# One more digit level in the expert routing, and all weight subtractions on GpSimd

## The chip, the cores and the metric

The kernel runs on one core of one Trainium2 chip. The metric is device time in microseconds from launch to end. A core has TensorE (matmuls, here PE, with PEld for its weight loads), VectorE (DVE), ScalarE (ACT), GpSimd (POOL) and SyncE (SP), which run their own queues in order and meet through semaphores; data sits in SBUF, matmuls write to PSUM, and sixteen DMA engines move data to and from HBM.

## The reference

Three stages, all in 32-bit floats. Attention over 4 batches, 8 heads, 768 positions with 64 dimensions, where a query sees the four first positions and the 128 last ones. Then a mixture of three projections, `h = max(x@w1, x@w2, x@w3)` and `h @ w_out` over 3072 tokens. Then eight experts of equal capacity, and the routing of tokens to them is what the change touches:

```python
logits = x @ w_gate                    # 3072 tokens, 8 experts
order = np.argsort(-logits.flatten())
for idx in order:                      # best bid first
    tok, e = idx // 8, idx % 8
    if assigned[tok] >= 0 or counts[e] >= cap: continue     # cap = 384
    assigned[tok] = e; counts[e] += 1
for e in range(8):
    mask = assigned == e
    out[mask] = np.maximum(x[mask] @ w1[e], 0) @ w2[e]      # 512 -> 1024 -> 512
```

## The kernel before

Matmuls run on the fp32r type, and exactness comes from splitting: each operand is a high part (a rounded copy, made by ScalarE) and a low part (source less high part), and a product is three matmuls, high by high, high by low and low by high. All high and low copies of weights are made in the kernel.

The attention and the first mixture (Attn and Moe1) fill the time to about 661 us. Then eight experts follow (Moe2). An expert works in eight slices of 128 hidden units. For each slice, `weights` (line 541) loads a quarter-megabyte slice of w1 into the staging tile sa and one of w2 into sb (two buffers each, loads issued on SyncE), ScalarE writes the high parts wah and wbh, and a subtraction on line 551 writes the low parts wal and wbl, into rings of six (`nring`). The counter `s.cv` sends the subtractions by turns to GpSimd and to VectorE: w1's (wal) always goes to GpSimd, w2's (wbl) to VectorE. Line 604 has the twelve matmuls of the first layer (into mm), lines 607 and 608 split its result into hh (ScalarE) and hl (VectorE), and line 597 has the nine matmuls of the second layer (into acc), one slice behind. After the eighth slice, three indirect DMAs on GpSimd's queue write the rows out (line 616).

The routing (Route) runs one expert at a time, in a chain. A phase finds the expert that fills up next, given what each free token bids for its best expert. It does so by a search over the 32 bits of the bid's sortable key, in digit levels, highest first: `SH` holds the shifts of the levels and `NZ` the number of values of each. In one level, VectorE compares each token's digit with all thresholds (`compare`, line 398, tile th, 24 columns of tokens by NZ thresholds), TensorE counts by expert in 24 small matmuls (`count`, line 404, weights ohr, into rc), VectorE compares the counts with the room left (met, line 448), a matmul merges the experts (line 450), VectorE adds up the digit (hit, line 451) and makes the next level's z (line 453), with w (line 444, line 445 in the last level) computed beside. Behind the levels, lines 454 to 498 settle who is taken (t1b, vt and others), and `slots` (line 505) turns the result into a list of rows idx. Then `fetch` (line 554) gathers the rows with three indirect DMAs on GpSimd's queue, and `turn` (line 565) transposes them on TensorE (pt, line 25). The first level's compare and count of a phase stand in `bids` (line 405), most of it for the first phase ahead of 661 us; seven phases run in all, six of them from 661 us on, and the eighth expert takes what is left (`last`).

What runs when is set by the framework's scheduler, which orders each engine's queue once, when the kernel is built. The routing steps are marked to go ahead of the work around them (by 300 or 400 places, `s1` and `s2`), so their instructions stand between the matmuls of the first experts. A step for expert n+2 is written ahead of expert n, and the transposes of expert n+1 ahead of slice 5 of expert n. No queue changes its order at run time.

Of the kernel before, what the change touches and what calls it, by code (L numbers as in the profile page):

```python
# [22 lines left out]
def f32(ap): return ap.bitcast(FT)  # L23
# [3 lines left out]
class Attn:  # L27
    def __init__(s, tc, q,k,v, keep, consts, pst, psp, pss, psv, work):
        s.tc=tc; s.nc=nc=tc.nc; s.q,s.k,s.v=q,k,v
        s.pst,s.psp,s.pss,s.psv,s.w=pst,psp,pss,psv,work  # L30
        jp=work.tile([128,128],I32,name="jp",tag="qs0",bufs=2)
        nc.gpsimd.iota(jp,pattern=[[1,128]],base=0,channel_multiplier=-1)
        s.ident=keep.tile([128,128],FR,name="ident")
        nc.vector.tensor_scalar(s.ident,jp,0.0,None,op0=OP.is_equal)
        s.ca=consts.tile([128,2,128],U8,name="ca")
        nc.vector.tensor_scalar(s.ca[:,0,:],jp,0.0,None,op0=OP.is_le)
        nc.vector.tensor_scalar(s.ca[:,1,:],jp,0.0,None,op0=OP.is_gt)
        s.ul=consts.tile([128,2,128],BF,name="ul")
        nc.vector.tensor_scalar(s.ul[:,0,:],jp,0.0,None,op0=OP.is_lt)
        nc.vector.tensor_scalar(s.ul[:,1,:],jp,0.0,None,op0=OP.is_ge)  # L40
        s.negs=consts.tile([128,2,4],FT,name="negs"); nc.vector.memset(s.negs,NEG)

        s.ps=consts.tile([128,160],FR,name="psn"); nc.vector.memset(f32(s.ps),0.0)
        s.vn=consts.tile([16,2,64],FT,name="vns"); nc.vector.memset(s.vn,0.0)
        s.vk=[]
        for i in range(2):
            t=consts.tile([128,2,128],FR,name=f"vk{i}"); nc.vector.memset(f32(t),0.0); s.vk.append(t)
        s.ks=consts.tile([128,2,64],FT,name="kss"); nc.vector.memset(s.ks,0.0)
        s.kf=[]; s.kz=[s.zeros([consts.tile([128,4,132],FR,name=f"kz{h}") for h in range(2)])]
        t=consts.tile([1,1],FT,name="one"); nc.vector.memset(t,0.0)  # L50
        nc.scalar.activation(t,t,AF.Exp)
        s.n=0; s.no=('kh0','kh1'); s.early=[]
        s.extra=None
        s.acc=lambda u: False
# [298 lines left out]
class Route:  # L353

    SH=(25,18,12,6,0); NZ=(128,128,64,64,64)
    M=128
    def __init__(s,tc,LG,pool,work,ps,cap=384):
        s.tc=tc; s.nc=nc=tc.nc; s.LG=LG; s.w=work; s.ps=ps; s.cap=cap  # L360
        c=pool; n=len(s.SH); V=nc.vector
        io=work.tile([128,192],FT,name="te")[:,0:128]
        nc.gpsimd.iota(io,pattern=[[1,128]],base=0,channel_multiplier=0,allow_small_or_imprecise_dtypes=True)
        s.thr=c.tile([128,128],BF,name="thr")
        V.tensor_copy(s.thr,io)
        pi=c.tile([128,1],FT,name="pcol"); s.pcol=pi
        nc.gpsimd.iota(pi,pattern=[[0,1]],base=0,channel_multiplier=1,allow_small_or_imprecise_dtypes=True)
        s.ones=c.tile([128,128],BF,name="onesb"); V.memset(s.ones,1.0)
        s.scale=c.tile([128,128],BF,name="scaleb"); V.memset(s.scale,128.0*8/s.M)
        s.tri=c.tile([128,128],BF,name="trib")  # L370
        V.tensor_scalar(s.tri,io,pi,1.0,op0=OP.is_ge,op1=OP.subtract)
        s.rank8=c.tile([128,8],FT,name="rank8")
        V.tensor_scalar(s.rank8,io[:,0:8],-1.0,8.0,op0=OP.mult,op1=OP.add)
        s.io8=c.tile([128,8],FT,name="io8"); V.tensor_copy(s.io8,io[:,0:8])
        s.io3=c.tile([128,3],FT,name="io3"); V.tensor_copy(s.io3,io[:,0:3])
        s.cp=c.tile([128,24,2],FT,name="cp")
        V.tensor_copy(s.cp[:,:,0],pi.to_broadcast([128,24]))
        V.tensor_copy(s.cp[:,:,1],io[:,0:24])

        po=c.tile([128,1],I32,name="pown"); pf=c.tile([128,1],FT,name="pownf")  # L380
        V.tensor_copy(po,pi); V.tensor_scalar(po,po,7,None,op0=OP.bitwise_and); V.tensor_copy(pf,po)
        s.own=c.tile([128,8],FT,name="own"); V.tensor_scalar(s.own,s.io8,pf,None,op0=OP.is_equal)
        s.sh=c.tile([128,n-1,24],I32,name="shifts"); s.mk=c.tile([128,n-1,24],I32,name="masks"); s.z24=c.tile([128,24],FT,name="z24"); V.memset(s.z24,0.0)
        for l in range(1,n):
            V.memset(s.sh[:,l-1,:],s.SH[l])
            V.memset(s.mk[:,l-1,:],127 if s.NZ[l]==128 else 63)
        s.R=c.tile([128,8],FT,name="room"); V.memset(s.R,float(cap))
        s.RP=c.tile([128,1],FT,name="roomp"); V.memset(s.RP,float(cap))
        s.UA=c.tile([128,24],FT,name="taken"); V.memset(s.UA,0.0)
        s.ASG=c.tile([128,24,8],BF,name="asg"); V.memset(s.ASG,0.0)  # L390
        s.ML=c.tile([128,24,8],FT,name="ml")
# [13 lines left out]
    def bids(s,r=(0,24),first=False):  # L405

        nc=s.nc; n=len(s.SH); V=nc.vector; a,b=r; m=b-a; C=slice(a,b)
        if a==0:
# [10 lines left out]
        V.tensor_tensor(key,key,bid.bitcast(I32),op=OP.bitwise_xor)  # L419
        V.tensor_scalar(s.D0[:,C],key,s.SH[0],s.NZ[0]-1,op0=OP.logical_shift_right,op1=OP.bitwise_and)  # L420
        V.tensor_copy(s.z[:,C],s.D0[:,C][:,:,None].to_broadcast([128,m,2]))
# [11 lines left out]
    def phase(s,bids=True):  # L433
        nc=s.nc; n=len(s.SH); V=nc.vector; M=s.M
        if bids: s.bids()
# [99 lines left out]
class Moe2:  # L535

    def __init__(s,tc,w1,w2,x2d,out,wpool,act,main,mm,acc,pt,ident,nring):
        s.tc=tc; s.nc=tc.nc; s.w1=w1; s.w2=w2; s.x2d=x2d; s.out=out
        s.wp=wpool; s.act=act; s.main=main; s.ng=0; s.mm=mm; s.acc=acc; s.pt=pt; s.ident=ident; s.nring=nring
        s.scat=[]; s.cv=0  # L540
    def weights(s,ev,f):
        nc=s.nc
        a=s.wp.tile([128,4,128],FT,name="sa",bufs=2); b=s.wp.tile([128,512],FT,name="sb",bufs=2)
        nc.sync.dma_start(a,s.w1[bass.ds(ev,1)].rearrange("a (k p) n -> p (a k) n",p=128)[:,:,f*128:(f+1)*128])
        nc.sync.dma_start(b,s.w2[bass.ds(ev,1)].rearrange("a f n -> (a f) n")[f*128:(f+1)*128,:])
        r=[]
        for nm,src in (("wa",a),("wb",b)):
            h=s.wp.tile(list(src.shape),FR,name=nm+"h",bufs=s.nring); l=s.wp.tile(list(src.shape),FR,name=nm+"l",bufs=s.nring)
            nc.scalar.activation(h,src,AF.Copy)  # L549
            s.cv+=1  # L550
            (nc.vector if s.cv%2==0 else nc.gpsimd).tensor_tensor(l,src,f32(h),op=OP.subtract)  # L551
            r.append((h,l))
        return r
    def fetch(s,idx,first=None):
# [191 lines left out]
```

## Time and profile before

| | us |
|---|---|
| median of 3 runs (1047.61 to 1052.12) | 1052.06 |
| the profiled execution | 1053.32 |
| its span, first to last instruction | 1051.5 |
| busy: TensorE / weight load / VectorE / ScalarE / GpSimd | 978.9 / 893.3 / 774.3 / 512.4 / 414.5 |
| mean granted TensorE clock | 0.977 of full |

Times are from the span's start. Matmuls are pipelined and the end of each is modelled, so a matmul's own duration overlaps the next one's, and what one costs is read from the distance of starts. A share of busy time is a mean over stages that have different limits, so the rows below are taken by stage. A wait is put down to the semaphore that came last.

### The profile page before, as it was taken

How to read it: one execution, taken by the hardware profiler on the slowest of the kernel's cores; microseconds unless marked ns; L12 is line 12 of the kernel's file. 1: busy time of each engine (PE TensorE's matmuls, PEld its weight loads, DVE VectorE, ACT ScalarE, POOL GpSimd, SP SyncE). 2: the span in 40 equal slices, each digit the busy share in tenths (PEclk: the TensorE clock that was granted, in tenths of full speed). 3: DMA queues.
4: the chain of work that ended last, by engine and by line, in shares of the span. 5: the costliest groups of instructions: out<-in, count | busy, mean ns of one | idle time of the engine just before them, and what ended most of it. 6: DMA issues, size and time to landing. Idle time of an engine off the chain costs nothing. (4 is left out here: it accounts for less than half of the span.)

```text
span 1051.5 us, 18670 instructions
## 1 busy us (share of the span) xinstructions
PE 978.9 (93%) x6682; PEld 893.3 (85%) x6682; DVE 774.3 (74%) x1822; ACT 512.4 (49%) x1166; POOL 414.5 (39%) x355
## 2 busy tenths in 40 slices
PE   6889999989999999999999999898978999899997
PEld 4658789989999999999999898777767778688896
DVE  6789976688888888988976526877868888763330
ACT  5775563577666666666664211423323333344441
POOL 2666635234444434444344000415334254272431
PEclk8899999999999999999999999989999999999999
DMA  5564421231121121122110000424234253364530
GB/s 136 132 169 138 141 58 49 70 100 46 42 56 47 45 71 41 39 70 46 42 41 2 1 1 31 148 83 146 91 110 153 71 160 102 120 207 119 156 100 31
DMA packets 148845, 89.61 MB, mean 85 GB/s; under 512 B 90160, under 2 KB 133680, under 8 KB 148752
## 3 DMA queue, kind: packets, MB, share of 16 engines
q1 hardware_dynamic: 144048, 74.39, 25.4%
q0 software_dynamic: 3840, 12.45, 3.6%
q10 hardware_dynamic: 864, 1.57, 0.4%
q8 instruction: 53, 0.87, 0.3%
q14 instruction: 40, 0.33, 0.1%
HBM read 74.76 MB, written 13.76 MB: 84 GB/s over the span
## 5 line engine op out<-in xcount | busy, mean ns | idle before, releaser
L551 POOL TENSOR_TENSOR wal<-sa,wah 128x512 fp32r<-128x512 f32 x64 | 89.1, 1393 | 204.1 <-ACT wah L549 198.3
L202 POOL TENSOR_TENSOR L<-A_w,H 128x768 fp32r<-128x768 f32 x46 | 87.2, 1895 | 140.2 <-ACT H L201 121.0
L317 PE MATMUL mm<-woh,hh 128*128 128x260 f32 (+1 forms) x288 | 83.3, 292 | 2.2 <-DVE LG L320 1.1
L549 ACT ACTIVATE wah<-sa 128x512 fp32r<-128x512 f32 x64 | 40.4, 631 | 91.6 <-PE mm L604 50.4
L317 PE MATMUL mm<-woh,hl 128*128 128x260 f32 (+1 forms) x288 | 82.4, 290 | 2.4 <-DVE hl L334 1.2
L317 PE MATMUL mm<-wol,hh 128*128 128x260 f32 (+1 forms) x288 | 82.3, 287 | 0.0
L298 DVE TENSOR_TENSOR hm<-mm,hm 128x384 f32<-128x384 f32 x96 | 53.1, 553 | 37.7 <-PE mm L295 36.7
L597 PE MATMUL acc<-wbl,hh 128*128 128x512 f32 x192 | 78.3, 408 | 0.0
L597 PE MATMUL acc<-wbh,hh 128*128 128x512 f32 x192 | 78.0, 406 | 0.1
L597 PE MATMUL acc<-wbh,hl 128*128 128x512 f32 x192 | 78.0, 406 | 0.0
L551 DVE TENSOR_TENSOR wbl<-sb,wbh 128x512 fp32r<-128x512 f32 x64 | 52.2, 818 | 32.8 <-ACT wbh L549 31.4
L549 ACT ACTIVATE wbh<-sb 128x512 fp32r<-128x512 f32 x64 | 40.3, 630 | 68.0 <-PE acc L597 55.7
L608 DVE SCALAR_TENSOR_TENSOR hl<-mm,hh 128x384 fp32r<-128x384 f32 x64 | 35.4, 554 | 50.9 <-ACT hh L607 47.6
L295 PE MATMUL mm<-xh,w0h 128*128 128x384 f32 x192 | 67.8, 353 | 2.3 <-DVE hm L298 1.1
L295 PE MATMUL mm<-xh,w1h 128*128 128x384 f32 x192 | 66.7, 347 | 1.7 <-DVE hm L298 0.9
L295 PE MATMUL mm<-xl,w0h 128*128 128x384 f32 x192 | 65.8, 342 | 0.8 <-DVE xl L285 0.8
L295 PE MATMUL mm<-xh,w2h 128*128 128x384 f32 x192 | 66.0, 344 | 0.3 <-ACT hm L297 0.3
L295 PE MATMUL mm<-xh,w2l 128*128 128x384 f32 x192 | 65.1, 339 | 0.0
L295 PE MATMUL mm<-xh,w1l 128*128 128x384 f32 x192 | 65.0, 338 | 0.0
L295 PE MATMUL mm<-xl,w1h 128*128 128x384 f32 x192 | 64.9, 338 | 0.0
L295 PE MATMUL mm<-xh,w0l 128*128 128x384 f32 x192 | 64.9, 338 | 0.0
L295 PE MATMUL mm<-xl,w2h 128*128 128x384 f32 x192 | 64.8, 338 | 0.0
(334 smaller groups left out, 3156.7 us busy)
## 6 DMA issues: line engine op xcount, KB each, us to landing
sa<-in_moe_w_dram SPq DMA_DIRECT2D x64, 256.0 KB
sb<-in_moe_w_dram SPq DMA_DIRECT2D x64, 256.0 KB
st<-in_moe_w_dram SPq DMA_DIRECT2D x18, 512.0 KB
qn<-in_q_dram SPq DMA_DIRECT2D x60, 96.0 KB
x2d<-xo SPq DMA_DIRECT2D x18, 256.0 KB
kn<-in_k_dram SPq DMA_DIRECT2D x32, 128.0 KB
st<-in_moe_w_out_dram SPq DMA_DIRECT2D x6, 512.0 KB
vn<-in_v_dram SPq DMA_DIRECT2D x24, 128.0 KB
```

The source lines that it names most:

```text
L202: nc.gpsimd.tensor_tensor(L,Af,f32(H),op=OP.subtract)
L295: nc.tensor.matmul(ps[:,:384],s.W[i][a][:,p,f*128:(f+1)*128],X[p][b],start=(n==0),stop=(n==11)); n+=1
L298: else: nc.vector.tensor_tensor(m,ps[:,:384],m,op=OP.max)
L317: nc.tensor.matmul(ps[:,:n],H[f][a][:,t*128:(t+1)*128],s.WO[b][:,f,u,:n],start=(k==0),stop=(k==17)); k+=1
L549: nc.scalar.activation(h,src,AF.Copy)
L551: (nc.vector if s.cv%2==0 else nc.gpsimd).tensor_tensor(l,src,f32(h),op=OP.subtract)
L597: nc.tensor.matmul(acc[t],H[f][a][:,t*128:(t+1)*128],W[f][1][b],start=(f==0 and n==0),stop=(f==F-1 and n==2)); n+=1
L608: nc.vector.scalar_tensor_tensor(l,ps[:,:384],0.0,f32(h),op0=OP.max,op1=OP.subtract)
```

## The change

The search goes from five levels of 7, 7, 6, 6, 6 bits to six of 6, 6, 5, 5, 5, 5 bits. The masks for the lower digits are computed from `NZ` instead of being chosen between 127 and 63. In `weights`, both subtractions of a slice go to GpSimd; the counter `s.cv` is gone.

```diff
-    SH=(25,18,12,6,0); NZ=(128,128,64,64,64)
+    SH=(26,20,15,10,5,0); NZ=(64,64,32,32,32,32)
...
-            V.memset(s.mk[:,l-1,:],127 if s.NZ[l]==128 else 63)
+            V.memset(s.mk[:,l-1,:],s.NZ[l]-1)
...
-        s.scat=[]; s.cv=0
+        s.scat=[]
...
             nc.scalar.activation(h,src,AF.Copy)
-            s.cv+=1
-            (nc.vector if s.cv%2==0 else nc.gpsimd).tensor_tensor(l,src,f32(h),op=OP.subtract)
+            nc.gpsimd.tensor_tensor(l,src,f32(h),op=OP.subtract)
```

## Rows read from the trace of the kernel before

**Rows 1.** Windows: stretch, length, busy PE PEld DVE ACT POOL (instructions), clock, DMA share, GB/s.

```profile
661.00:940.00 279.00, 248.61 (x1971) 212.05 (x1971) 227.07 (x649) 94.70 (x182) 111.59 (x83) 0.95 0.40 123
...
939.50:974.50 35.00, 35.00 (x181) 31.19 (x180) 12.18 (x21) 16.39 (x32) 13.42 (x11) 1.00 0.49 148
```

**Rows 2.** TensorE's waits, 661 to 940 us: us in total, times, longest.

```profile
PE rc L450 <- DVE met L448: 10.4, 7, 3.4
PE pt L25 <- DMA xg<-x2d,idx: 6.2, 5, 2.7
PE rc L526 <- DVE vt L522: 5.5, 7, 2.3
PE rc L404 <- DVE th L398: 3.5, 3, 1.9
PE rc L493 <- DVE t1b L472: 2.6, 3, 0.9
```

**Rows 3.** Timeline (start, us): VectorE at two subtractions, GpSimd and TensorE at the second.

```profile
672.27 2.47 DVE L551 TENSOR_TENSOR wbl<-sb,wbh 128x512 fp32r<-128x512 f32 x1
...
896.01 1.24 DVE L551 TENSOR_TENSOR wbl<-sb,wbh 128x512 fp32r<-128x512 f32 x1 [2.08 <-ACT wbh L549]
897.18 0.34 DVE L448 TENSOR_SCALAR met<-rc,roomp 128x128 bf16<-128x128 f32 x1
...
896.97 1.42 POOL L551 TENSOR_TENSOR wal<-sa,wah 128x512 fp32r<-128x512 f32 x1 [0.26 <-ACT wah L549]
...
897.57 0.22 PE L450 MATMUL rc<-met,scaleb 128*128 128x128 bf16 x1 [3.38 <-DVE met L448]
```

**Rows 4.** VectorE by form, 661 to 940: xcount | busy us, mean ns | idle before.

```profile
L551 DVE TENSOR_TENSOR wbl<-sb,wbh 128x512 fp32r<-128x512 f32 x45 | 39.0, 871 | 8.6 <-ACT wbh L549 7.2 <-issue 1.3
L398 DVE TENSOR_TENSOR th<-z,thr 128x3072 bf16<-128x3072 bf16 x12 | 23.2, 1934 | 0.2
...
L445 DVE TENSOR_SCALAR w<-z 128x24 f32<-128x24 bf16 x6 | 1.6, 272 | 0.0
```

**Rows 5.** Line 551, 661 to 940: ns min/median/max, first and last start.

```profile
L551 POOL TENSOR_TENSOR wal<-sa,wah x46: 1267/1296/2717, 661.7 to 937.9; 128x512 fp32r<-128x512 f32 x46
...
L551 DVE TENSOR_TENSOR wbl<-sb,wbh x45: 676/685/2470, 671.3 to 938.0; 128x512 fp32r<-128x512 f32 x45
```

**Rows 6.** A wait of ScalarE, 661 to 940 us, as in rows 2.

```profile
ACT wah L549 <- PE mm L604: 35.8, 16, 4.9
```

**Rows 7.** Timeline: a VectorE operation and the GpSimd subtraction beside it.

```profile
689.88 1.25 DVE L453 TENSOR_SCALAR z<-w,digit 128x48 bf16<-128x48 f32 x1
...
689.78 1.31 POOL L551 TENSOR_TENSOR wal<-sa,wah 128x512 fp32r<-128x512 f32 x1 [0.37 <-ACT wah L549]
```

**Rows 8.** Timeline of VectorE in the first routing step, levels 1 to 3.

```profile
637.60 0.25 DVE L453 TENSOR_SCALAR z<-w,digit 128x48 bf16<-128x48 f32 x1
637.88 1.76 DVE L398 TENSOR_TENSOR th<-z,thr 128x3072 bf16<-128x3072 bf16 x1
...
642.28 0.25 DVE L453 TENSOR_SCALAR z<-w,digit 128x48 bf16<-128x48 f32 x1
642.56 0.96 DVE L398 TENSOR_TENSOR th<-z,thr 128x1536 bf16<-128x1536 bf16 x1
...
645.33 0.25 DVE L453 TENSOR_SCALAR z<-w,digit 128x48 bf16<-128x48 f32 x1
```

**Rows 9.** Timeline of TensorE in the first routing step: two counts.

```profile
639.70 1.50 PE L404 MATMUL rc<-th,ohr 128*128 128x128 bf16 x24
...
643.57 0.86 PE L404 MATMUL rc<-th,ohr 128*128 128x64 bf16 x24
```

**Rows 10.** A stretch's clock (columns as rows 1); chain: start, us, what.

```profile
897.80:901.20 3.40, 3.40 (x18) 3.09 (x18) 2.08 (x6) 0.00 (x0) 0.59 (x1) 0.50 0.75 236
...
897.79 3.21 PE mm L604 x10
...
950.42 2.12 PE mm L604 x12
```

## The prediction

> **What bounds the kernel now.** I read the windows first, cut at the starts of the write-outs of the eight experts. From 661 to 940 us, where the first five experts run beside the routing, TensorE is busy 248.6 of 279 us at a mean clock of 0.95; the two experts after it need 35.0 us each with TensorE busy for all of them at 1.00 [rows 1]. So the last three experts are bound by TensorE alone, and nothing that VectorE or GpSimd do there can show unless it becomes late. The first five take 279 us; five at 35 would take 175, and the routing's own matmuls, the gathered tokens' transposes and the tail of the layer before account for part of the rest. What is lost there is 30.4 us of idle TensorE and the time at the lower clock.
>
> Next the waits of TensorE in that stretch [rows 2]: it waits for VectorE to compare the counts (met, 10.4 us in 7 waits), for VectorE's vt, th and t1b (5.5, 3.5 and 2.6 us), and for gathered rows (6.2 us). All but the last are links of the routing chain on VectorE, which runs its queue in order. Then the timeline at the longest wait [rows 3]: VectorE stands on wbl, a weight subtraction whose input is not there yet (2.08 us idle, then 1.24 us), met comes behind it, and TensorE idles 3.38 us. The wbl subtractions themselves never starve TensorE in the rows of waits; it is what queues behind them that does.
>
> **Weights to GpSimd: what leaves VectorE.** 45 wbl in the stretch are 39.0 us of busy time and 8.6 us of idle ahead of them [rows 4]; one takes 0.685 us (the median [rows 5]) but the mean is 0.871. Four of the waits for met have a wbl right in front of met: the one of 3.38 us, one where the subtraction took 2.47 us [rows 3], and two like it near 681 and 812 us. I count 7 of the 10.4 us as theirs (ends 3.4, the one shown whole, and 10.4, all): **-7 us**.
>
> **What arrives at GpSimd.** The same operation takes 1.296 us there (median, 46 in the stretch) [rows 5]. 45 more are 58 us on an engine busy 111.6 of 279, so it comes to about 170. In a later expert it is busy 13.4 of 35 us and gets 8 x 1.30 = 10.4 more: 24 of 35 [rows 1]. That costs nothing there, because both halves of the weights stand in rings of six slices and ScalarE waits for the matmuls to free a slot (35.8 us in 16 waits [rows 6]): the ring is full, some five slices of over 4 us ahead. If that cover went, each late slice would stop TensorE for as long as it is late. Two things queue behind the moved instructions. The gather of the next tokens stands in GpSimd's queue, so it can start up to one subtraction (1.3 us) later, and TensorE waited for gathers five times in this stretch [rows 2]: 0 to +6.5 us, I take **+1.5**. The load of the next w2 slice on SyncE waits for the moved subtraction to free its staging buffer (two of them); the full ring hides this too.
>
> **What GpSimd does to VectorE.** A VectorE operation that starts inside a GpSimd subtraction waits until that ends: z of 48 elements took 1.25 us beside a subtraction of 1.31 us [rows 7], and 0.25 us in the first routing step, when GpSimd subtracts nothing [rows 8]. The operations by form in the stretch [rows 4], against their clean times, give the sum: th of 3072 elements 12 x (1.934 - 1.76) = 2.1 us, and so on over 13 forms (the first and the last stand there) down to w of line 445, 0.6: 22 us, or 22 / 46 = 0.49 us for each present subtraction, besides 8.4 us on wbl itself, 45 x (0.871 - 0.685), which leave with it. 45 more at that price are +22 us of VectorE time (ends 0 and 45 x 1.30 = 58: no overlap at all, and a full block each time). I take 22, since it is the same operation in the same place. On TensorE I price it by the waits whose VectorE operation is stretched so: t1b 2.6, the longest for vt, 2.3, and those for th without the longest, 3.5 - 1.9: 6.5 us together [rows 2]. As many subtractions again: **+6.5** (0 to +13).
>
> The Trainium skill, GPSIMD Engine Reference, section 4.1 (Engine selection), says that two-input elementwise work should go to VectorE, GpSimd being about half as fast; here 1.296 against 0.685 us agrees. Its section 1 (Specifications) says that the SBUF interfaces are shared, with contention for VectorE instructions with two SBUF inputs; z and the forms above agree in effect. By that rule the move loses time, and it is the first rival below.
>
> **The digits.** Before, a phase compares and counts 128, 128, 64, 64, 64 thresholds; after, 64, 64, 32, 32, 32, 32. VectorE's compare is 1.76 us for 3072 elements and 0.96 for 1536 [rows 8]; on that line 768 take 0.96 - 0.40 = 0.56 (an estimate; not below half of 0.96 and not above it). A phase: 2 x 1.76 + 3 x 0.96 = 6.40 becomes 2 x 0.96 + 4 x 0.56 = 4.16, so -2.24. The added level's small operations: a 64 level alone lasts 645.33 - 642.28 = 3.05 us, of which the compare is 0.96 and the count on TensorE 0.86, so at most 1.23 is VectorE's. Net -1.0 a phase, -6 in the six phases of the stretch. TensorE's 24 count matmuls are 1.50 us for 128 columns and 0.86 for 64 [rows 9]; for 32 I take 0.86, since weights are loaded 24 times all the same (not above that, and not below half). A phase: 2 x 1.50 + 3 x 0.86 = 5.58 becomes 6 x 0.86 = 5.16, less 0.1 back for one more small matmul: -0.3, **-2 us** in six (to -12 with half). The added level is one more exchange between the two engines: the waits for met and th are (10.4 + 3.5) / 30 = 0.46 us a level, and six more levels are +2.8; as most of met's share leaves with wbl, **+2** (0 to +5). As a chain the levels behind the first stay even: 4.68 + 3 x 3.05 = 13.8 us before, 3.05 + 4 x (3.05 - 0.40) = 13.7 after [rows 8].
>
> **What follows.** VectorE's account in the stretch: -39 - 8.6 + 22 - 6 = -32 of 279 us. The idle time of TensorE that is neither wbl's nor the gathers', 30.4 - 7 - 6 = 17 us, is mostly waits for VectorE's queue; how much of it a queue shorter by 11% gives back is the widest unknown, 0 to 17. I take a third, **-6**. After several stalls the clock was granted at half for 3.4 us: at 0.50 ten matmuls took 3.21 us where twelve take 2.12 at full clock [rows 10], 1.4 us lost each time; two such stretches fewer and one new: **-1.5**. Initial weights, the routing setup and everything up to 661 us: 0; the masks and shifts grow by one row of 24, and the attention and the first mixture hold none of the edited lines.
>
> Sum: -7 + 1.5 + 6.5 - 2 + 2 - 6 - 1.5 = -6.5 us. The profiled execution took 1053.32 us with a span of 1051.5 (1.8 us lie around it), 1.3 us over the median of 1052.06; on it the sum gives 1046.8, on the median 1045.6. **I predict 1045.5 us**, and for this case 1036 to 1050.
>
> **The rivals.** *GpSimd blocks VectorE* (slower): if an added subtraction costs VectorE more than (39 + 8.6 + 6) / 45 = 1.19 us, the account turns positive; 0.49 is measured now, but subtractions twice as dense meet fewer free operations, and w2's follow w1's closely. At 1.30 the 58 us replace 22: VectorE +4 us instead of -32, no -6 from the queue, the stalls cost +13 instead of +6.5, and the digits' part stays: -7 + 1.5 + 13 - 2 + 2 = +7.5, so 1058 to 1060. Against it: operations that read PSUM are not stretched (met took 0.34 us inside a GpSimd subtraction of 1.42 us [rows 3]). *The edits cancel*: what wbl gives back the sixth exchange and the later gathers take, and the critical path moves to the routing chain, which is as long as before: 1052, from 1047 to 1056. For it: levels of equal length. *Much more is given back*: all of the 17 us, with two more clock stretches: 1031. *The change doesn't do what it says*: the digits still make 32 bits and the ring and order of weights stay, so only the schedule around could shift; 1052.
>
> **Chances.** Forecast 0.53; cancel 0.21; GpSimd blocks 0.19; much more 0.05; not what it says 0.02. About 0.5%, 5.3 us, is what a measurement of this kernel can tell from no change. The forecast's own range puts 0.45 under 1046.8 and 0.08 within the bound; cancel puts 0.19 within and 0.02 above. Faster 0.50, same 0.29, slower 0.21. The range from 1033 to 1060 leaves out under 0.2.
>
> **What would show it.** Right: line 551 gone from VectorE, 128 on GpSimd at 1.3 us; TensorE's waits for met well under 10 us although there are more levels; VectorE busy about 30 us less from the first expert to the fifth; the last three experts unchanged at 35 us. Wrong: z, w, vt and te at means over twice their clean times, TensorE's waits for vt, th and t1b above 20 us, waits of matmuls for wbl, gathers queued behind subtractions, or compares of 32 thresholds near 0.96 us.

## The result, and the profile after

The changed kernel takes 1059.22 us (median of 16 runs), beside 1049.01 us for the kernel before (16 runs on the same chip): a ratio of 1.0101, 95% interval 1.0078 to 1.0123. It is slower by 1%. That is over the forecast's own range, 1036 to 1050, and inside the wide one, 1033 to 1060, on the other side than forecast. The time is near the one worked out for the first rival, 1058 to 1060; as a change it is +10.2 us where that rival's sum was +7.5, since the kernel before takes 3 us less over 16 runs than over the three known then. The profiled execution took 1058.42 us with a span of 1056.6. That is 5.1 us over the profiled one of before, half of the difference of the medians: the stages below tell where time went and by what, and the medians how much.

The busy times, from the page of after (share of the span, instructions):

```profile
PE 975.5 (92%) x6857; PEld 888.7 (84%) x6857; DVE 751.6 (71%) x1802; ACT 512.1 (48%) x1166; POOL 490.6 (46%) x419
```

VectorE lost 22.7 us of work and GpSimd took 76.1 us on, as the change says. Nothing in this line is an engine at its limit that was not before, so the time has to be looked for by stage. The windows of after run from the first gather to the fifth expert's write-out, then over the two experts behind it; the columns are those of [rows 1].

```profile
665.30:944.80 279.50, 241.13 (x2072) 203.11 (x2072) 211.33 (x626) 89.19 (x170) 156.41 (x123) 0.94 0.39 117
...
944.80:980.20 35.40, 35.38 (x183) 31.54 (x182) 6.69 (x12) 16.77 (x33) 23.60 (x19) 1.00 0.45 141
980.20:1015.30 35.10, 35.08 (x182) 31.25 (x181) 6.69 (x12) 16.46 (x32) 23.51 (x19) 1.00 0.46 143
```

The same first stage of the kernel before, which begins and ends at other times:

```profile
667.60:939.40 271.80, 242.89 (x1922) 207.05 (x1922) 221.35 (x634) 89.76 (x170) 107.94 (x80) 0.95 0.40 121
```

The late experts stand where they stood in [rows 1], at 35 us, although GpSimd has 24 us of work in each instead of 13: the rings hide it. All of the loss between these two executions lies in the routing stage, 279.5 against 271.8 us, although it began 2.3 us earlier. TensorE is busy 1.8 us less there and idle 38.4 us instead of 28.9, at a mean clock of 0.94 instead of 0.95. So the stage has less work and more stops. Their releasers are in the waits of TensorE in that stage (us in total, times, longest), to be held against [rows 2]:

```profile
PE rc L526 <- DVE vt L522: 11.4, 6, 4.6
PE rc L404 <- DVE th L398: 8.6, 5, 3.6
PE rc L493 <- DVE t1b L472: 7.1, 6, 1.4
PE acc L596 <- DVE hl L607: 5.9, 2, 4.0
PE rc L450 <- DVE met L448: 1.9, 2, 1.5
...
PE acc L579 <- DMA xg<-x2d,idx: 1.1, 2, 0.8
```

The waits for met went from 10.4 to 1.9 us, as forecast. Those for vt, th and t1b went from 11.6 to 27.1 us together, over the 20 us that the prediction named as a sign against it, and hl of the second layer is a new one. (Line numbers behind the edit are one lower in after: the subtractions are line 550.)

VectorE's forms in that stage show what made vt, th and t1b late (xcount, busy us, mean ns, idle before), and below them line 550 (ns min/median/max):

```profile
L453 DVE TENSOR_SCALAR z<-w,digit 128x48 bf16<-128x48 f32 x36 | 19.8, 550 | 1.2
L398 DVE TENSOR_TENSOR th<-z,thr 128x768 bf16<-128x768 bf16 x24 | 15.5, 646 | 0.8
...
L529 DVE SCALAR_TENSOR_TENSOR idx<-idf 128x3 int32<-128x3 f32 x7 | 8.1, 1156 | 0.1
L517 DVE TENSOR_SCALAR uv<-qi 128x24 int32<-128x24 int32 x7 | 7.3, 1046 | 0.1
...
L445 DVE TENSOR_SCALAR w<-z 128x24 f32<-128x24 bf16 x6 | 3.7, 610 | 0.0
```

```profile
L453 DVE TENSOR_SCALAR z<-w,digit x36: 239/248/4646, 670.6 to 893.8; 128x48 bf16<-128x48 f32 x36
...
L550 POOL TENSOR_TENSOR wal<-sa,wah x64: 1259/1296/2582, 658.1 to 1021.4; 128x512 fp32r<-128x512 f32 x64
L550 POOL TENSOR_TENSOR wbl<-sb,wbh x64: 1262/1293/2272, 660.2 to 1026.5; 128x512 fp32r<-128x512 f32 x64
```

A subtraction costs GpSimd the 1.30 us that [rows 5] had. z's mean of 550 ns is over twice its median of 248, with one of 4646 ns among 36; w of line 445 went from 272 [rows 4] to 610 ns. An average hides how this time is spread. Here is the longest, in the timelines of VectorE, GpSimd and TensorE:

```profile
670.63 4.65 DVE L453 TENSOR_SCALAR z<-w,digit 128x48 bf16<-128x48 f32 x1
675.19 0.28 DVE L325 TENSOR_TENSOR hl<-mm,hh 128x128 fp32r<-128x128 f32 x1
675.39 0.94 DVE L398 TENSOR_TENSOR th<-z,thr 128x1536 bf16<-128x1536 bf16 x1
```

```profile
669.24 1.00 POOL L561 DMA_INDIRECT xg<-x2d,idx  x1 [0.30 <-issue]
670.27 1.29 POOL L550 TENSOR_TENSOR wal<-sa,wah 128x512 fp32r<-128x512 f32 x1
671.50 1.28 POOL L550 TENSOR_TENSOR wbl<-sb,wbh 128x512 fp32r<-128x512 f32 x1
672.72 1.29 POOL L550 TENSOR_TENSOR wal<-sa,wah 128x512 fp32r<-128x512 f32 x1
673.96 1.26 POOL L550 TENSOR_TENSOR wbl<-sb,wbh 128x512 fp32r<-128x512 f32 x1
```

```profile
676.39 0.86 PE L404 MATMUL rc<-th,ohr 128*128 128x64 bf16 x24 [2.44 <-DVE th L398]
```

After a gather (an indirect DMA, the first line of GpSimd's), it had four subtractions waiting and ran them without a gap. z, a quarter of a microsecond of work, began beside the first and ended as the last ended, at 675.2. th came behind it, and TensorE stopped for 2.44 us. At 741.73 us much the same happens to uv (line 517, 4.32 us): it begins while GpSimd issues a write-out and ends with the last of three subtractions behind it. hl of the second layer stands behind it in VectorE's queue, and TensorE stops for 3.96 us in an expert's matmuls.

To compare kernels I call **stretch** the time that VectorE's operations of a stage took beyond the fastest tenth of their own form, summed. Before it is 34.1 us, beside 44 subtractions that GpSimd begins in the stage, and 8.6 of it are on wbl itself; after it is 58.0 us beside 87, of which six single operations hold 20.8 us.

### The profile page after: what moved, and what is told of

Read it like the earlier page. It is cut to its first block, busy times and chain, and to the rows that moved or that the text cites. A ratio compares the mean times of both kernels' runs of the same rounds, so it can differ in the third digit from the quotient of the medians.

```text
span 1056.6 us, 19036 instructions
## 1 busy us (share of the span) xinstructions
PE 975.5 (92%) x6857; PEld 888.7 (84%) x6857; DVE 751.6 (71%) x1802; ACT 512.1 (48%) x1166; POOL 490.6 (46%) x419
## 4 chain that ended last, share of the span: by engine, by line
PE 57%; DVE 25%; issue 6%; ACT 5%; DMA 3%; POOL 2%; SPq 0%; POOLq 0%; DVEq 0%; ACTq 0%
PE mm L295 20%; PE mm L603 9%; PE acc L596 8%; PE mm L317 5%; PE rc L404 3%; PE pt L25 2%; PE po L206 2%; DVE th L398 2%; DMA st<-in_moe_w_dram 2%; DVE A_w L188 1%; PE pp L25 1%; DVE cA L250 1%; DVE z L453 1%; PE ps L139 1%; PE ps L142 1%
## 5 line engine op out<-in xcount | busy, mean ns | idle before, releaser
L550 POOL TENSOR_TENSOR wal<-sa,wah 128x512 fp32r<-128x512 f32 x64 | 86.5, 1355 | 89.8 <-ACT wah L549 89.7
L550 POOL TENSOR_TENSOR wbl<-sb,wbh 128x512 fp32r<-128x512 f32 x64 | 85.0, 1328 | 68.4 <-ACT wbh L549 68.2
```

Of the source, the lines that this page charges most:

```text
L550: nc.gpsimd.tensor_tensor(l,src,f32(h),op=OP.subtract)
```

## The experiments

Two theories stood: that GpSimd's subtractions hold up VectorE, and that the added digit level costs more than shorter compares give. Each diff is against the changed kernel unless it says otherwise. Ratios are to the kernel before on the same chip; stages and windows are cut as above, in the one profiled execution of each kernel.

**The edits apart.** Six levels, with the subtractions by turns as before:

```diff
-        s.scat=[]
+        s.scat=[]; s.cv=0
...
-            nc.gpsimd.tensor_tensor(l,src,f32(h),op=OP.subtract)
+            s.cv+=1
+            (nc.vector if s.cv%2==0 else nc.gpsimd).tensor_tensor(l,src,f32(h),op=OP.subtract)
```

> Six digit levels, and the weight subtractions by turns on GpSimd and VectorE as before. Theory A (the added GpSimd subtractions hold VectorE's operations, the digits are harmless): at or under the kernel before, 1042 to 1050 us against 1049, VectorE's operations stretched no more than before (z mean about 0.36 us). Theory B (the sixth level costs the time through one more exchange between VectorE and TensorE per phase): most of the loss is here, 1055 to 1060 us, with longer waits of TensorE for met and th.

Measured: 1036.54 us, ratio 0.9864 (0.9828 to 0.99). And the other edit alone, five levels with all subtractions on GpSimd:

```diff
-    SH=(26,20,15,10,5,0); NZ=(64,64,32,32,32,32)
+    SH=(25,18,12,6,0); NZ=(128,128,64,64,64)
...
```

> Five digit levels as before, all weight subtractions on GpSimd. Theory A: the whole loss is here, 1057 to 1064 us; single small VectorE operations last 2.5 us or more beside two to four subtractions in a row; TensorE's waits for vt, th and t1b above 20 us. Theory B: 1045 to 1051 us.

Measured: 1081.03 us, ratio 1.0266 (1.0217 to 1.0315). -1.4% and +2.7% make +1.3%, beside +1.0% for both: the edits nearly add up, and the small total was two large terms. The stage and the waits of TensorE with the digits alone, and then with GpSimd alone:

```profile
663.10:922.70 259.60, 234.88 (x2073) 196.18 (x2072) 204.86 (x672) 90.64 (x171) 103.08 (x81) 0.97 0.42 127
```

```profile
PE rc L450 <- DVE met L448: 6.6, 6, 2.9
PE rc L526 <- DVE vt L522: 6.4, 5, 3.6
PE acc L580 <- DMA xg<-x2d,idx: 3.0, 2, 2.6
PE rc L404 <- DVE th L398: 2.9, 4, 0.9
...
PE pt L25 <- DMA xg<-x2d,idx: 0.9, 1, 0.9
```

```profile
668.40:968.10 299.70, 248.46 (x1916) 212.00 (x1915) 225.93 (x589) 88.51 (x170) 169.08 (x123) 0.92 0.37 109
```

```profile
PE rc L526 <- DVE vt L522: 15.4, 6, 5.3
PE rc L404 <- DVE th L398: 10.8, 6, 3.6
PE rc L493 <- DVE t1b L472: 7.6, 5, 2.8
PE rc L450 <- DVE met L448: 6.9, 4, 6.2
```

With the digits alone the stage is 12.2 us shorter than before, TensorE busy 8.0 us less and idle 4.2 us less. With GpSimd alone it is 27.9 us longer: 22.3 us more idle, and the clock at 0.92. No matmul of either waits for a weight's low part (wal, wbl), so it is not GpSimd's own lateness that stops TensorE. VectorE's stretch is 28.0 us in the one and 62.3 in the other, with seven operations holding 22.0 of it. The theory that the added level costs time fell here. The theory of holds keeps its sign, but both sizes are beyond what was expected of it.

**No subtraction on GpSimd.** Six levels, all of them on VectorE:

```diff
-            nc.gpsimd.tensor_tensor(l,src,f32(h),op=OP.subtract)
+            nc.vector.tensor_tensor(l,src,f32(h),op=OP.subtract)
```

> Six digit levels, all weight subtractions on VectorE, none on GpSimd, so nothing holds VectorE's operations but itself. From 655 to 940 us VectorE gains about 88 subtractions of 0.69 us (61 us) and loses the 61 us by which its operations are stretched in the changed kernel. Theory A: every small operation at its clean time (z 0.25, w 0.18), the subtractions at 0.69, and 1050 to 1060 us, level with the changed kernel or under it. Theory B, in which VectorE's length is not the matter but the exchanges are: at or over the changed kernel, 1059 to 1070.

Measured: 1036.94 us, ratio 0.9871 (0.9836 to 0.9907). And none at all: ScalarE writes zeros in place of the low parts, so all that the weights' low parts add to a product is left out.

```diff
-            nc.gpsimd.tensor_tensor(l,src,f32(h),op=OP.subtract)
+            nc.scalar.activation(l,src,AF.Copy,scale=0.0)
```

> The changed kernel with each low part of the expert weights written as zero by ScalarE (a copy with scale 0) in place of the subtraction: that part of the result is left out, and neither GpSimd nor VectorE has any work for it. ScalarE has 128 more operations of 0.63 us. Theory A: the subtractions' whole price comes out, 1030 to 1042 us, VectorE's operations at clean times. Theory B: 1052 to 1058, since the exchanges are all there.

Measured: 1019.29 us, ratio 0.9704 (0.9669 to 0.9739). The stages of the two, and z with all subtractions on VectorE:

```profile
660.20:913.40 253.20, 230.80 (x2023) 193.56 (x2022) 202.16 (x700) 90.31 (x171) 33.67 (x30) 0.97 0.40 123
```

```profile
L453 DVE TENSOR_SCALAR z<-w,digit x36: 239/248/249, 671.5 to 901.9; 128x48 bf16<-128x48 f32 x36
```

```profile
666.20:912.00 245.80, 231.16 (x2072) 196.50 (x2072) 158.65 (x627) 133.70 (x260) 36.68 (x37) 0.97 0.44 133
```

With all subtractions on VectorE no z of 36 takes over 249 ns (395 with none at all), and the stretch is 3.7 us (3.2 with none at all). That shows the cause of the stretch: the same 36 operations, with no subtraction on GpSimd beside them. And the subtractions themselves are cheap on VectorE: 43.5 us more work in the stage (202.16 less 158.65) for 17.7 us of time. On GpSimd they add 52.7 us to VectorE's busy time over none (211.33 less 158.65) and cost some 42 us (1.0101 less 0.9704, of 1050). (The kernel with none has 43.4 us more of ScalarE's work in the stage, whose price no run shows.) I had expected the kernel with all of them on VectorE to be slower than before; it is faster.

**How the price grows with the number.** Only w1's low parts are made, on GpSimd; those of w2 are zeros from ScalarE, so what they add to the second layer's product is left out:

```diff
...
-            nc.gpsimd.tensor_tensor(l,src,f32(h),op=OP.subtract)
+            s.cv+=1
+            if s.cv%2==0: nc.scalar.activation(l,src,AF.Copy,scale=0.0)
+            else: nc.gpsimd.tensor_tensor(l,src,f32(h),op=OP.subtract)
```

> Six digit levels; w1's low parts by GpSimd as in every version, w2's low parts written as zero by ScalarE, so that part of the result is left out. It stands between no subtraction at all (1019 us) and the changed kernel (1059), with 64 of its 128 GpSimd subtractions. If each GpSimd subtraction has the same price: half way, 1039 us. If the price rises with density, because subtractions that run one behind the other hold VectorE for their sum: well under half way, 1026 to 1034 us, and no small VectorE operation over 2.5 us. And against digits_alone (1037) it tells what w2's subtractions cost on VectorE.

Measured: 1024.63 us, ratio 0.9774 (0.973 to 0.9819), stretch 26.0 us.

```profile
662.10:911.10 249.00, 231.22 (x2073) 195.61 (x2072) 179.56 (x627) 111.43 (x214) 97.90 (x81) 0.97 0.43 132
```

The first 64 subtractions on GpSimd cost 5 to 7 us over none (by medians, by ratios). The second 64 cost 34 us more on GpSimd (1.0101 less 0.9774) and 9 to 12 us on VectorE (the digits alone less this kernel). So the price is not proportional to the number, which my sum had assumed. One operation, a w that began during a gather, still lasted 3.03 us, where I had expected none over 2.5.

To see whether it is the place, the same 64 on GpSimd as both subtractions of every second slice; the other slices' low parts are zeros:

```diff
...
-            nc.gpsimd.tensor_tensor(l,src,f32(h),op=OP.subtract)
+            s.cv+=1
+            if (s.cv-1)%4<2: nc.gpsimd.tensor_tensor(l,src,f32(h),op=OP.subtract)
+            else: nc.scalar.activation(l,src,AF.Copy,scale=0.0)
```

> Six digit levels and 64 GpSimd subtractions, as many as in w1_only (1025 us), but both of every second slice; the low parts of the other slices are written as zero by ScalarE, so that part of the result is left out. If the number of subtractions sets the price: 1023 to 1027 us. If it is their standing one behind the other: more than w1_only, 1028 to 1038 us, with small VectorE operations of about 2.6 us (two subtractions in a row).

Measured: 1025.31 us, ratio 0.9774 (0.975 to 0.9797), the same. But only three pairs of the stage ran one behind the other without a gap, as many as with w1's alone. So it says that at this number the place does not matter, and does not test what a run of subtractions costs.

Cutting each subtraction in two halves of 256 columns lets VectorE in twice as often:

```diff
-            nc.gpsimd.tensor_tensor(l,src,f32(h),op=OP.subtract)
+            lv,sv,hv=(x if len(x.shape)==2 else x.rearrange('p k n -> p (k n)') for x in (l,src,f32(h)))
+            for c in (slice(0,256),slice(256,512)): nc.gpsimd.tensor_tensor(lv[:,c],sv[:,c],hv[:,c],op=OP.subtract)
```

> The changed kernel with each GpSimd subtraction in two halves of 256 columns, one behind the other. If VectorE gets the SBUF port back at the end of each GpSimd instruction, a small VectorE operation waits at most for half a subtraction, about 0.7 us, and the kernel gains: 1045 to 1056 us. If VectorE waits as long as GpSimd's queue holds work that is ready, the two halves hold it as one and their fixed cost comes on top: 1059 to 1072 us, with z and w as long as before.

Measured: 1054.14 us, ratio 1.0039 (1.0011 to 1.0066): 5 to 7 us under the changed kernel (by medians, by ratios), with a stretch of 49.0 us. The longest hold stayed; this z began in the middle of a run of halves, at 678.83 us:

```profile
L453 DVE TENSOR_SCALAR z<-w,digit x36: 239/249/4659, 672.1 to 894.3; 128x48 bf16<-128x48 f32 x36
```

Shorter instructions help a little, but a run of subtractions can still be waited for as a whole. This run settles neither theory of the long holds.

**The hold by itself.** The digits-alone kernel with a measurement put ahead of the attention, in the first 31 us of its 1078.19: GpSimd gets 1, 2, 4 subtractions (and 4 halves) in a row, while VectorE runs 40 additions of 24 elements, from SBUF, and once more from PSUM.

```diff
+    J=[(1,512,a),(2,512,a),(4,512,a),(4,256,a),(4,512,p[:,0:24])]
...
+        for i in range(n):
...
+            nc.gpsimd.tensor_tensor(o[:,0:width],S[j][:,0:width],S[j][:,0:width],op=OP.subtract)
...
+        for i in range(40): V.tensor_tensor(o[:,i],src,c,op=OP.add)
```

> digits_alone with a measurement ahead of the attention, of use only by its trace (some 30 us longer): VectorE runs 40 additions of 24 elements behind one another, five times; at the start of each the GpSimd gets subtractions that are all ready: one of 512 columns, two, four, four of 256 columns, and four of 512 while VectorE's additions read PSUM and SBUF. If VectorE gets the port back at the end of each GpSimd instruction: one addition of about 1.3 us for each GpSimd subtraction, the others 0.16. If it waits as long as GpSimd has work ready: one addition of 1.3, of 2.6 and of 5.1 us, and of some 2.8 us beside the four narrow ones. With PSUM as a source: none over 0.3 us.

Its additions by form (ns min/median/max), then the groups of 40 beside 1, 2 and 4 subtractions and, last, the one with the PSUM operand, in VectorE's timeline:

```profile
L633 DVE TENSOR_TENSOR bv<-ba,bc x160: 164/169/1047, 4.2 to 27.3; 128x24 f32<-128x24 f32 x160
L633 DVE TENSOR_TENSOR bv<-bp,bc x40: 160/161/166, 27.5 to 31.0; 128x24 f32<-128x24 f32 x40
```

```profile
4.23 4.67 DVE L633 TENSOR_TENSOR bv<-ba,bc 128x24 f32<-128x24 f32 x40
...
8.92 5.57 DVE L633 TENSOR_TENSOR bv<-ba,bc 128x24 f32<-128x24 f32 x40
...
14.51 7.30 DVE L633 TENSOR_TENSOR bv<-ba,bc 128x24 f32<-128x24 f32 x40
...
27.46 3.66 DVE L633 TENSOR_TENSOR bv<-bp,bc 128x24 f32<-128x24 f32 x40
```

With the PSUM operand 40 additions take 3.66 us although four subtractions run beside them. From SBUF they take 1.0, 1.9 and 3.6 us more beside 1, 2 and 4: each subtraction holds one addition, for at most 1.05 us, and VectorE gets one addition in between two subtractions. The Trainium skill, "SBUF — State Buffer", section "Who interferes with whom", says that the port pair the two engines share is locked for the whole instruction and not split; a hold of 1.05 us beside a subtraction of about that length, and none with the PSUM operand, agree. It has no hold that outlasts one instruction, such as z's 4.65 us. The measurement does not show one either, so why a whole run is sometimes waited for stays open.

The trace of the changed kernel shows one thing that the measurement lacked. In its stage GpSimd ran two or more subtractions without a gap 12 times. Six of these runs were waited for to their end by one operation, those with the 20.8 us; in four VectorE waited for one subtraction at a time, and in two nothing was held. All six stood right behind an indirect DMA on GpSimd's queue, a gather or a write-out, and four of the six operations began while it ran. In the only two runs with a held operation and no indirect DMA ahead, no operation waited for more than one. With GpSimd alone there are six more such waits, all behind an indirect DMA. It is no rule: two runs behind gathers in the changed kernel let VectorE in after the first subtraction, and the z of 4.66 us in the kernel with halves began well behind its gather. An indirect DMA ahead of the subtractions was not tested by itself. Nor were operations like z and uv, which read one tensor from SBUF where the additions read two.

**What the digits gain.** Eight levels of 16 values, subtractions by turns:

```diff
-    SH=(26,20,15,10,5,0); NZ=(64,64,32,32,32,32)
+    SH=(28,24,20,16,12,8,4,0); NZ=(16,16,16,16,16,16,16,16)
```

> As digits_alone, but eight levels of 4 bits (16 thresholds each). If the gain of six levels is the shorter compares and counts, two more levels bring little more: a phase's compares go from 4.16 to about 2.8 us, and the two added levels bring back about 2.4 us of small operations, so VectorE +1 us a phase and 1036 to 1043 us against 1037. If an added level costs an exchange that TensorE feels (0.46 us or more, and clock), 1043 to 1052.

Measured: 1044.96 us, ratio 0.9959 (0.9937 to 0.9981). The stage is 259.6 us, as with six levels; the first gather comes at 669.0 instead of 663.1 us. In the first routing step, which runs undisturbed, the seven steps from level to level are 2.30 us each, 16.1 us; with six levels they are 3.07 and four of 2.53 (13.2 us), before 4.68 and three of 3.05 (13.9 us). From 64 to 32 thresholds a level gets 0.5 us shorter, from 32 to 16 only 0.2, and each further level adds 2.3; of five, six and eight levels, six make the shortest chain behind the first level.

Then six levels with every compare made twice as long as the count needs (the counts stay 64 and 32 wide), subtractions by turns:

```diff
-        s.compare(s.z,s.NZ[0],OP.is_ge,s.TH,r)
+        s.compare(s.z,2*s.NZ[0],OP.is_ge,s.TH,r)
...
-                s.count(pc,s.compare(z,k,OP.is_ge),k)
+                s.count(pc,s.compare(z,2*k,OP.is_ge),k)
```

> As digits_alone, but VectorE compares twice as many thresholds as TensorE counts (128, 128, 64, 64, 64, 64), so a phase's compares last 2 x 1.76 + 4 x 0.96 = 7.36 us against 4.16, some 20 us of VectorE more over the phases; the counts and the exchanges stay. If digits_alone gained 14 us by the shorter VectorE queue: the gain is gone, 1047 to 1056 us. If it gained by the shorter counts on TensorE: 1037 to 1043.

Measured: 1052.65 us, ratio 1.003 (1.0005 to 1.0056). Its stage, TensorE's waits for gathered rows in it, its compares, and the compares with the digits alone:

```profile
665.20:935.90 270.70, 236.37 (x1994) 196.31 (x1993) 215.83 (x649) 89.49 (x168) 104.06 (x75) 0.94 0.38 116
```

```profile
PE pt L25 <- DMA xg<-x2d,idx: 10.7, 7, 2.2
...
PE acc L580 <- DMA xg<-x2d,idx: 5.0, 2, 3.8
```

```profile
L398 DVE TENSOR_TENSOR th<-z,thr 128x1536 bf16<-128x1536 bf16 x24 | 23.9, 998 | 0.8
L398 DVE TENSOR_TENSOR th<-z,thr 128x3072 bf16<-128x3072 bf16 x12 | 21.6, 1802 | 0.2
```

```profile
L398 DVE TENSOR_TENSOR th<-z,thr 128x768 bf16<-128x768 bf16 x24 | 15.3, 639 | 0.7
...
L398 DVE TENSOR_TENSOR th<-z,thr 128x1536 bf16<-128x1536 bf16 x12 | 12.5, 1044 | 0.2
```

The compares grew by 17.7 us in the stage (45.5 against 27.8) and by 21.0 in the whole kernel (47.2 to 68.2 on line 398), the kernel by 16 to 17 us and the stage of these two executions by 11.1. So a microsecond of compares cost about 0.8 of time. The waits that grew most are those for gathered rows, the end of the routing chain: 15.7 us beside 3.9 with the digits alone, while those for met and th stayed. This puts the price on the length of the chain, and most of what the digits bring is the shorter compares on it. That the shorter counts bring nothing is not shown: the compares here are also 3.9 us longer in the stage than in the kernel before (41.6), with one level more.

**A version from this.** Six levels; the first five experts' subtractions all on VectorE, where the routing runs, and by turns in the last three, where VectorE has room and no routing stands behind:

```diff
...
-            nc.gpsimd.tensor_tensor(l,src,f32(h),op=OP.subtract)
+            s.cv+=1
+            (nc.vector if s.cv<=80 or s.cv%2==0 else nc.gpsimd).tensor_tensor(l,src,f32(h),op=OP.subtract)
```

> Six digit levels; the subtractions of the first five experts, beside which the routing runs, all on VectorE, those of the last three by turns as before. By theory A it joins the first 913 us of vector_all with experts of 35 us after: 1032 to 1037 us, under digits_alone and vector_all (both 1037). By a theory that the place of the subtractions does not matter, 1037 or over.

Measured: 1031.57 us, ratio 0.9837 (0.9797 to 0.9877): the lowest median of those that compute everything, faster than both kernels. Its interval overlaps those of the digits alone and of all subtractions on VectorE. Its stage:

```profile
663.60:913.40 249.80, 233.68 (x2024) 196.06 (x2023) 201.53 (x695) 90.52 (x171) 42.20 (x37) 0.95 0.41 126
```

If the price grows with the number, a few on GpSimd should be cheaper still. So, in the first five experts, every second of w1's goes there:

```diff
...
-            nc.gpsimd.tensor_tensor(l,src,f32(h),op=OP.subtract)
+            s.cv+=1
+            (nc.gpsimd if s.cv%4==1 or s.cv>80 and s.cv%2 else nc.vector).tensor_tensor(l,src,f32(h),op=OP.subtract)
```

> As vector_first5 (1032 us), but in the first five experts w1's subtraction of every second slice goes to GpSimd: 20 there, 60 on VectorE. In w1_only 40 single subtractions on GpSimd cost little (64 in all, 5 us over none), and 40 on VectorE cost about 12 (digits_alone less w1_only). So a single GpSimd subtraction is the cheaper place: 1027 to 1032 us. If two VectorE subtractions and one on GpSimd disturb each other as in digits_alone: 1032 to 1037.

Measured: 1038.52 us, ratio 0.9884 (0.9845 to 0.9923), above what was expected, with runs from 1027.8 to 1042.1. The interval overlaps that of the version above, so no gain, and a loss that can't be told from none.

## Why the prediction was wrong

**Right.** The waits for met: 10.4 to 1.9 us where 7 us were taken off. The rings hide the moved work in the late experts, and the three of them end as fast as before [rows 1, 6]. The gathers did not suffer: waits for gathered rows fell from 6.2 to 1.1 us where I put +1.5. With the digits alone the compares of the stage shrank by 13.8 us (41.6 to 27.8), beside 13.4 forecast.

**The step that gave the wrong sign: what GpSimd does to VectorE.** I took 0.49 us of VectorE for each present subtraction, "since it is the same operation in the same place", and on TensorE the 6.5 us of waits a second time. Measured, the forms other than wbl went from 25 to 58 us of stretch, +33 instead of +22, and the waits for vt, th and t1b rose by 15.5 us, and those for hl by 5.9, instead of 6.5 in all. Three things failed. The place was not the same: w2's subtraction follows w1's on one queue, and behind a gather or a write-out up to four ran without a gap. The mean per subtraction hid that six operations carry 20.8 of 58.0 us, and the long ones are those seen to stop TensorE, for 2.44 and 3.96 us above. And the price is not proportional: 64 on GpSimd cost 5 to 7 us over none, the next 64 cost 34. For this edit my terms came to -7 + 1.5 + 6.5 - 6 = -5 us; alone it is +28.

**The queue relief, -6 us.** VectorE's account was to fall by 32 us; its busy time in the stage fell by 10.0 (221.35 to 211.33), since what wbl left the holds took. A shorter account could not help when single operations of 4 us stand in it: TensorE's idle time rose by 9.5 us. The deciding point that I gave for the first rival, 1.19 us of VectorE per added subtraction, was the wrong one for the same reason. The account never turned positive, and yet the rival's time came. It is the stops of TensorE that set the time, not VectorE's total.

**The digits, mis-sized.** With -2 for the counts, +2 for the exchange and 6 of the 32 us in the queue relief, I had about -1 us; alone they are -14.5. TensorE's counts, taken by the median distance of their starts, fell from 28.7 to 22.8 us (-5.9, with 25 ns for a matmul at 32 columns, 29 at 64 and 56 at 128), against -2 taken and -12 as the far end. The failed step is where I put the compares: as load in a queue of which a third comes back. They are links of the chain from level to level, and there 21.0 us of compares cost 16 to 17 us. My own chain of levels gave 13.8 against 13.7 us, and the undisturbed first step shows 13.9 against 13.2. Both leave out the first level, which went from 128 thresholds to 64: by [rows 8] and [rows 9] its compare fell from 1.76 to 0.96 us and its count from 1.50 to 0.86. With these 1.4 us and the 0.7 behind it a phase is 2.1 us shorter, some 13 us in six phases (an estimate), near the 14.5.

**The clock, -1.5.** It went the other way, as the stops did: the mean clock of the stage is 0.95 before, 0.94 after, 0.97 with the digits alone and 0.92 with GpSimd alone, where TensorE is idle 28.9, 38.4, 24.7 and 51.2 us.

So the mechanism of the first rival, to which I gave 0.19, was at work beside a gain that I had put at a tenth of its size. The GpSimd edit alone lies far outside the range, at 1081 us; the digits' gain brought the two together back into it. A range that holds the time with two wrong terms in the sum is luck, and only the runs with one edit each could show it. The Trainium skill, GPSIMD Engine Reference, section 4.1 (Engine selection), which gives two-input elementwise work to VectorE because GpSimd is about half as fast at it, had the direction, though not this reason: with all subtractions on VectorE the kernel is 2.3% faster than after.

What stays open: why some operations wait for a whole run of subtractions and others for one, and so how much of the non-proportional price is runs and how much is number. Every edit also gives the scheduler other queues to order, and no run separates that from the edit itself.

## What to carry to other kernels

Price a move to another engine by what the moved instruction does to its neighbour's shortest operations, and look at the longest hold, not at the mean: a 0.25 us link of a chain that waits 4.65 us costs TensorE, a long operation that is planned for costs little. Ask of each microsecond whether it lies on a chain from engine to engine or in a queue with slack: here one of compares cost about 0.8 us of time (16 to 17 for 21.0), one of planned subtractions 0.4 (17.7 us for 43.5). When a change has two edits, give each its own sum, since a small total can be the difference of two large terms.

## What the runs showed of the hardware that I had not expected

- A VectorE operation of 48 elements can stand for a whole run of GpSimd subtractions: 4.65 us for four of 1.29 us, and 4.66 us when each was cut in two. In the measurement by itself it never was more than one, 1.05 us. The six such waits of the changed kernel all stood right behind an indirect DMA of GpSimd; why is open.
- An operation that reads one operand from PSUM was not held at all: 160 to 166 ns beside four subtractions.
- Counts of 32 columns start 25 ns apart and those of 64 columns 29 ns: below 64 columns a matmul here gets hardly cheaper (25 ns at 16 columns too, with eight levels).
